# Weight conversion without its clamp, a second load of the weights that checks it, and x of two chunks turned together on VectorE

## The chip, the cores and the metric

One core of one Trainium2 chip. The metric is the device time of one execution in microseconds; the median over several executions is compared with the median of the changed kernel.

## What is computed

A linear recurrence with decay over 768 steps gives x, and a block that mixes over time and then over channels turns x into the output. Everything is float32.

```
r, k, v: (4, 8, 768, 48) = 0.1 * randn      w: the same shape, 0.8 + 0.15 * rand     u: (8, 48)
U: (768, 32)   V: (32, 768)   w_ch1: (384, 1536)   w_ch2: (1536, 384)

for t in range(768):
    y[t]  = r[t] @ (state + (u * k[t]) v[t]^T)
    state = w[t][:, None] * state + k[t] v[t]^T
x = y as (4, 768, 384)
h = x^T @ U @ V;   a = x + h^T;   out = a + relu(a @ w_ch1) @ w_ch2
```

## The kernel before

The 768 steps of each of the four batches are cut into six chunks of 128 steps, 24 chunks (g = 0 to 23) in all. For a chunk, VectorE runs two scans over the decays (steps F and Q), scales r and k by them (RP, KS), TensorE forms the 128 x 128 scores of every head (AM), VectorE merges them under the triangular mask into A (CP), and TensorE multiplies with v (YA) and with the state that the chunk inherits (YZ). ScalarE copies y to a block buffer xT (XE). The state goes on through DS (TensorE), ZA (VectorE) and ZM. For the mixing over time each chunk's x is needed transposed: for chunks 0 to 11 TensorE transposes it (XT, XN), for chunks 12 to 23 VectorE does it in 32 x 32 blocks (XD, 16 instructions of 32 x 96 for a chunk, line 676); k is turned the same way (KD, 16 instructions of 32 x 128).

When a batch's six chunks are there, GA, G4, SELM, GS, GSL form the small product with U, HP multiplies with V, UADD adds it to x, and UH and UL split the sum into a high and a low part, each of which fits TensorE's rounded 32-bit format (fp32r). The feed-forward part runs over seven blocks of 384 or 512 columns (WIDTHS). A block has 12 UP groups (line 826) and 12 DN groups (line 860) of nine matmuls each: high times high, low times high, high times low. HH and HL (lines 831, 833, 837) make the high and low part of the hidden rows, O (875) adds the result, OUT (878) stores it.

The weights come as 64-bit numbers, 27 pieces: U, V in two halves, and 12 pieces each of w_ch1 and w_ch2 (384 KB a piece). The pair of 32-bit words of a number is turned into one float32 by `split_raw`: AB takes the absolute value of the high word (ScalarE, line 271), E scales the low word (ScalarE, 288), C1 clamps (VectorE, 293), C2 shifts (300), C3 puts the sign back (307), ADD adds the low word (GpSimd, 314), HI and SUB split the result into high and low part (324, 331). Data that fall outside what the fast path can do are told by flags (`guard`, `tots`): PW, PC, PD reduce them, PF reads the flag, and a slow general path would follow the fast one.

All of this is a list of 1415 steps. The order in which they are given out, and for some of them which of two engines takes them, is a written-out string, ORDER: each step has a number, and its third digit says the engine and how many idle matmuls TensorE gets before the step (`lead`; line 186). Each engine takes its instructions in that order and waits where data are not there. SyncE issues all loads and stores, in order too. Buffers come from pools with a number of places (20 in `big`, 3 in `ffn`, and so on); a load waits until its place is free.

In this order the first batch's six chunks and the conversion of the first weights come first, then GA to UL of the first block, then UP 0.3. From there the chunks of later batches run between the matmul groups of earlier blocks.

Of the kernel before, what the change touches and what calls it, by code (L numbers as in the profile page):

```python
# [8 lines left out]
F32 = mybir.dt.float32  # L9
# [41 lines left out]
def channel_order():  # L51
# [25 lines left out]
    "2L02T02o06d06e09U0A602X02h02Z02U06+06-02M12p02Y02a09L07M07102V19602b02r07N0AF07002g09S12s02i09h09W09m02j09V0"
    "2k02q03407209T12t09702c07Q07402x02l07309p07502d07609X02m09Y02e19813M02u09n02y09b02v09o19c09i02n13603503D09d0"
    "2+02w19y0C109e09u1A903709f07702-03E03802z09Z07A03909v19w03F09a13003103203G07R03A07B09x09z0780AH13B0CA03H0A10"
    "7O0A203I07U03V03313e07V03N07S07C0AB03J0A303X03C17P1A703W03K07W07T13Y03L1AC03g07D07X1AY08S13P03Q0AE13O0AD0A40"  # L80
    "7G07b03Z09+0AO03R07c0AA13f03S0AI03a03T0C207d0A807E07k03U17Y0AJ07H0Cf03b07l0Ai07m07e0A503c07F03h03i0CB03d1Ah0"
    "7Z0C403j0Ab0AM07I03k07f1AK1AZ0AL17a07t0Ad07g03l0Aj17n0790Cg03m17u0Ae0CV0CC07J07v0CD0AP07o07z07p0C909-07K07w0"
    "D907+0AN0CH0Ak07L07h0Al0AT0C60Ag0A01Am1AU0Af0Ao0Ch0CI0Ac0C707-0CE07x0CJ0AQ0C81An0CW0AV0C307y0AW0Ap0CF07i07j0"
    "Aa0Ci0AR07q0860C-0CY0CK0CZ0800AS1AX0Aq0DA1Ce0Ca0811Ar0Cd0As07r0820Cl0CN0C51D00DB0CG0CL0Cb0CO1D80Cc1At0DC0CM0"
    "Ef08308707s0D20Cj0CP0Au0Av0840Aw0Ax0Cm0DV0D70Cp0Ay0CX0Ck1DY0Az0Cn0Df0880Eg0850D408908C0Cq08D0Co0CQ0Cr0Dg1D50"
    "Cu0De0DW0Dd0E00D30Da0Cv0D61A+0D-0Dh0Dl0Cs0Db0Di08A0A-08E0E20B30B008F0Hg0B10DZ1B40DF0E708I0B70Dm08J0B80DG0Ct1"
    "DH0E40EW0B20E90B50DD1E31Dc1D108K0Ig0B60DE0B90E10BA08L0Cw0E80Dj1EV0DI0BW0E50DL0DJ08M0Dn08G0DM0BK0BL0Cx0BB0E61"
    "8B0EY0BX0JA0BC0Ea0DK0EA0Dk0BM0EZ1Eh0Dp0EB0DO0Eb0EF0DN1DP0BH0BY08H0Dq0JB0BI0Do0Ec1BD0CR0Bc0Bd0BT0BJ08N0EG0Hh0"
    "Hi0H30EC0BN0Hj0ED0H20Be0DQ0Ee0BO0DX0Dr0EH0Cy0BP0EJ0EE0Ds0Ed0H50BU0Du0BV0Ei0Dv0Dt1BE0BQ0Ej0BZ0Dw0EK0DR0EI0BR0"
    "EL0CS0DS0Ih0H61BF0EM0EO0Ba0Bb0EX0EP0Dx0DT0HW0El0BG0Bi0EN1Ek0H70JC0Bf0EQ0Dy0HC0BS0ER0Bg0HA0IA0Em0Bl0Bj0Ii0En0"  # L90
    "HB0Eo0HZ0HD0HX0Ep0Bm0Bh0Bn0CT0H80Bk0Bo0ES0Dz0I00Eq0Ha1Cz0Br0ET0Hk1Er0DU0CU0Bs0Bp0Bt0IB0He0Es0Et0Bu0D+0C+0EU0"
    "HE0Bx0Eu0HI0Ev0Hf0By0H40Ew0HF0Ex0I30HJ0Ey0Ez0H91Bz0E+0HG1I40Bv0F20E-0F30HM0F00F40I90F60B+0F11F70F80F51F91Hb0"
    "HH0IC1B-0HY0FG0Hc0FM0Bw0FN0HN0FA0FH1Hl0FO0ID0FB0FI0Fb0Hm0FV0Jg0I10FW0I50IE0FC0Fc1Ij0Hd1HK0FD0FE0Fd0FX0FJ0HL0"
    "HO0IF0JD0IW0HP1HQ0FF0Bq0Hn0FK0Hq0IZ0G00I80C00FS0FT0I60FL0Hr0I71HR0FU0G10Ho0Fh0FP0IG0FQ0Fi0Hv0Hw0Jh0Hp0Fj0G21"
    "Hs0IK0Fe0Hx0Ib0Fk0FR0Hy0IH0IX0Ff0IL0If0Ic0FY0Fg0FZ0Ia1Ie0JY0I20Fa0G30Fl0Ik0Im0In0Fm0J00Fn0JW0Ji1Fq0Fo0Il0Fr0"
    "JE0J10Fs0II0G40IJ0Ft0Id0G50Jj0J30G80Fw0Ht0G90G60J50Hu1GA0J60Fu0Iq0IM0G71GB1J40IP0Fv0J80IY0IQ0IR0Hz0Io0IN0HS0"
    "Fx0GC0JG0Fy0JZ0Fz0JH0GX0Fp0GD0Ip0JI0Jk0IO1GY0F+0GR0J70F-0Ir0GZ0J90GS0GE0GU0Is0JF1JK0Iv0Jl1Iw0GT0H+0Jb0HT0Jf0"
    "GI0Ix0IS0H-0Iy0GV0JL0GF0GW0Gd0Ge0GJ1It0GK0Jc0Iu1J20GL0Iz0GG0JX0Gf0Je1Jd1JJ0GO0JM0JP0JQ0GP1GH0GQ0Ja1Jm0GM1Ga0"
    "IT0Jn0JN0GN0HU0JR0Gb1Gg0JO1Gc0Gj0IU0Jo0I+0HV0Jp0Gk1I-0Gh0Jq0Gl0Gi0JS0JT0IV0Gm0Jr0Gn0Go0Gp0Js0JU0JV0Gs0Gt0Jt0"
    "Jv0Ju0Jw0Gu0Gq0Jx0Jy0Gv0Jz0J+0Gy0J-0Gw0K00Gz0K30K11K70K40K20G+0K80K50L10L20K90K60G-0KA1H00Ki0Kj1KN0KZ0Kk0KO0"  # L100
# [7 lines left out]
class Buf:  # L108


    def __init__(self, pool):
        self.pool, self.left = pool, 0
# [20 lines left out]
def plan(steps, caps):  # L133


    order, taken, done = [], dict.fromkeys(caps, 0), set()
    for n in range(0, len(ORDER), 3):
        i, how = DIGITS.index(ORDER[n]) * 64 + DIGITS.index(ORDER[n + 1]), DIGITS.index(ORDER[n + 2])
        s = steps[i]
        assert s not in done and done.issuperset(s.after), s.name  # L140
        if how % 2:
            s.eng = s.alt
        s.lead = how // 2
        for buf in s.take:
            taken[buf.pool] += 1
            assert taken[buf.pool] <= caps[buf.pool], s.name
        for buf in s.bufs:
            buf.left -= 1
            taken[buf.pool] -= not buf.left
        done.add(s)  # L150
        order.append(s)
    assert len(order) == len(steps)
    return order
# [3 lines left out]
def rwkv_moe_kernel(ctx, tc, wT, rkT, vN, vS, rkN, uB, uT, uD, U, V, w1, w2, out):  # L157
# [7 lines left out]
    psF = pool("psF", 3, space=PSUM)  # L165
    dram = pool("dram", 1, space=DRAM)
    big = pool("big", BIG_BUFS)
# [953 lines left out]
```

## Time and profile before

| | us |
|---|---|
| median of 3 runs | 464.66 |
| lowest, highest | 462.23, 464.88 |
| the profiled execution | 463.0 |
| its span, first to last instruction | 461.1 |

The profiled execution lies 1.66 us under the median of the runs; 1.9 us of its time lie outside the span. PE is TensorE's matmuls, PEld its weight loads, DVE VectorE, ACT ScalarE, POOL GpSimd, SP SyncE.

### The profile page before, as it was taken

The page shows a single profiled execution, that of the slowest core. Times are in us where ns is not written, and L with a number is a line of the kernel's source. Part 1 is how long each engine was busy: PE and PEld are TensorE (multiplying, and loading weights), DVE is VectorE, ACT ScalarE, POOL GpSimd, SP SyncE. Part 2 cuts the span into 40 slices and gives each one's busy share as a digit, 9 for nine tenths or more (in the row PEclk, how much of TensorE's full clock was granted, in tenths as well). Part 3 has the DMA queues.
Part 4 walks back from the last instruction along what each step waited for, and adds up shares of the span by engine and source line. Part 5 has one row for each costly group of instructions (what it writes and reads, how often), then busy time and mean ns, then how long its engine had stood idle before and what let it go on. Part 6 is the DMA issues. An engine that isn't in the chain of part 4 may idle for free.

```text
span 461.1 us, 9867 instructions
## 1 busy us (share of the span) xinstructions
PE 438.8 (95%) x3917; PEld 371.7 (81%) x3917; DVE 365.3 (79%) x813; ACT 182.0 (39%) x494; POOL 114.2 (25%) x146
## 2 busy tenths in 40 slices
PE   5997998999999979999999999999999999999994
PEld 2776757898999869777786878887877689999994
DVE  8999789999899989999999999689999545313400
ACT  4888678989654425224302232023330002101200
POOL 1221225423275456645402322210000010000000
PEclk9586599999999999999999999999999999999998
DMA  8994724443755445502211321220200000010002
GB/s 277 282 344 149 253 74 139 150 168 118 228 156 185 138 161 181 160 21 81 83 62 30 143 67 47 67 66 25 67 1 1 23 17 8 0 41 17 2 0 75
DMA packets 20213, 47.38 MB, mean 103 GB/s; under 512 B 2432, under 2 KB 7296, under 8 KB 20160
## 3 DMA queue, kind: packets, MB, share of 16 engines
q1 hardware_dynamic: 20160, 46.67, 31.3%
q8 instruction: 33, 0.54, 0.5%
q14 instruction: 20, 0.16, 0.1%
HBM read 41.94 MB, written 4.72 MB: 101 GB/s over the span
## 4 chain that ended last, share of the span: by engine, by line
PE 58%; DVE 29%; ACT 4%; DMA 4%; issue 3%; SPq 1%; POOL 0%; ACTq 0%; DVEq 0%
PE f L860 22%; PE f L826 22%; DVE xn L676 9%; DVE kn L676 4%; DVE hid L837 3%; DMA raw_w<-in_w 2%; DVE F L379 2%; DVE A L547 2%; PE y L614 2%; DVE Q L392 1%; PE dS L556 1%; PE y L624 1%; PE aps L542 1%; DMA w<-in_wT 1%; PE aps L534 1%
## 5 line engine op out<-in xcount | busy, mean ns | idle before, releaser
L826 PE MATMUL f<-u,w1h 128*128 128x384 f32 (+1 forms) x504 | 150.6, 368 | 1.6 <-DVE hid L837 1.5
L860 PE MATMUL f<-hid,w2h 128*128 128x384 f32 (+1 forms) x504 | 149.8, 367 | 0.0
L826 PEld LDWEIGHTS f<-u,w1h 128*128 128x128 f32 x504 | 93.2, 188 | 15.1 <-DVE hid L837 3.0
L860 PEld LDWEIGHTS f<-hid,w2h 128*128 128x128 f32 x504 | 93.3, 188 | 12.3 <-issue 2.3
L860 PE MATMUL f<-hid,w2l 128*128 128x384 f32 (+1 forms) x252 | 91.5, 363 | 0.0
L826 PE MATMUL f<-u,w1l 128*128 128x384 f32 (+1 forms) x252 | 91.4, 363 | 0.0
L831 ACT ACTIVATE hid<-f 128x384 fp32r<-128x384 f32 (+1 forms) x69 | 36.0, 534 | 117.1 <-PE f L826 109.7
L837 DVE SCALAR_TENSOR_TENSOR hid<-f,hid 128x384 fp32r<-128x384 f32 (+1 forms) x84 | 50.1, 607 | 19.5 <-ACT hid L831 18.7
L676 DVE STREAM_TRANSPOSE xn<-xT 32x96 f32<-32x96 f32 x192 | 51.7, 269 | 2.7
L860 PEld LDWEIGHTS f<-hid,w2l 128*128 128x128 f32 x252 | 47.4, 188 | 5.0
L826 PEld LDWEIGHTS f<-u,w1l 128*128 128x128 f32 x252 | 47.4, 188 | 4.4
L676 DVE STREAM_TRANSPOSE kn<-rk 32x128 f32<-32x128 f32 x160 | 48.3, 302 | 2.4
L314 POOL TENSOR_TENSOR cva_w<-cva_w,raw_w 128x384 int32<-128x384 int32 x24 | 28.0, 1175 | 86.0 <-DVE cva_w L307 32.2
L446 ACT ACTIVATE A<-ident,dv 128x128 f32<-128x128 f32 x120 | 37.7, 391 | 1.0 <-DVE dv L491 0.8
L875 DVE TENSOR_TENSOR xT<-f,xT 128x384 f32<-128x384 f32 (+1 forms) x21 | 12.8, 608 | 26.8 <-PE f L860 26.6
L392 DVE TENSOR_TENSOR_SCAN Q<-w,qd 128x516 f32<-128x516 f32 x24 | 30.7, 1277 | 0.2
L379 DVE TENSOR_TENSOR_SCAN F<-w,resets 128x517 f32<-128x517 f32 x24 | 29.5, 1231 | 0.5 <-DMA w<-in_wT 0.4
L453 POOL TENSOR_SCALAR_AFFINE_SELECT A<-dv 128x128 f32<-128x128 f32 (+1 forms) x54 | 16.8, 348 | 42.9 <-DVE dv L432 36.9
L787 ACT ACTIVATE u<-xT 128x384 fp32r<-128x384 f32 (+1 forms) x18 | 10.0, 568 | 40.0 <-DVE xT L782 24.6
L793 POOL TENSOR_TENSOR u<-xT,u 128x512 fp32r<-128x512 f32 (+1 forms) x8 | 9.2, 1153 | 60.6 <-DVE u L789 49.0
L594 ACT ACTIVATE Z<-Z,tots 128x96 f32<-128x96 f32 x64 | 18.6, 363 | 13.4 <-DVE Z L585 13.4
L399 POOL TENSOR_TENSOR rk<-rk,Q 128x512 f32<-128x512 f32 x10 | 11.9, 1190 | 48.2 <-DVE Q L392 44.7
(114 smaller groups left out, 574.2 us busy)
## 6 DMA issues: line engine op xcount, KB each, us to landing
rk<-in_rkT SPq DMA_DIRECT2D x24, 512.0 KB, 5.2
raw_w<-in_w SPq DMA_DIRECT2D x24, 384.0 KB, 4.3
kr<-in_rkN SPq DMA_DIRECT2D x18, 384.0 KB, 3.8
w<-in_wT SPq DMA_DIRECT2D x24, 258.5 KB, 3.0
v<-in_vS SPq DMA_DIRECT2D x24, 224.0 KB, 3.7
out_dram<-xT SPq DMA_DIRECT2D x12, 192.0 KB, 3.3
out_dram<-xT SPq DMA_DIRECT2D x9, 256.0 KB, 2.9
raw_V<-in_V SPq DMA_DIRECT2D x6, 96.0 KB, 6.0
```

The costliest lines, as they stand in the source:

```text
L314: lambda: nc.gpsimd.tensor_tensor(out=d["to"].bitcast(I32), in0=d["a"].bitcast(I32), in1=d["e"], op=ALU.add),
L379: nc.vector.tensor_tensor_scan(out=F[:, ::-1], data0=st["w"][:, ::-1], data1=resets[:, ::-1], initial=1.0, op0=ALU.mult, op1=ALU.add)
L392: nc.vector.tensor_tensor_scan(out=st["Q"], data0=st["w"][:, 0:n], data1=qd, initial=0.0, op0=ALU.mult, op1=ALU.add)
L446: nc.scalar.activation(to, one, AF.Copy, scale=dv[:, NP * i + j : NP * i + j + 1])
L453: nc.gpsimd.affine_select(out=A[:, i, js, ts], in_=dv[:, NP * i + js.start : NP * i + js.stop].unsqueeze(2).broadcast_to([P, NQ, n]), patt ...
L594: nc.scalar.activation(st["Z"][:, j], src[:, j], AF.Copy, scale=nxt[:, j : j + 1])
L676: nc.vector.transpose(a, b)
L826: nc.tensor.matmul(ps, wt[:, f, ct, :], u[ct][:, z], start=(m == 0), stop=(m == 8))
L831: nc.scalar.activation(h[:, 0], d["ps", f], AF.Relu)
L837: nc.vector.scalar_tensor_tensor(out=h[:, 1], in0=d["ps", f], scalar=0.0, in1=h[:, 0].bitcast(F32), op0=ALU.max, op1=ALU.subtract)
L860: nc.tensor.matmul(d["o", ct], wt[:, 4 * ct + part, f - 3 * part, :], hid[f][:, z], start=(part == 0 and m == 0), stop=(part == 3 and m == 8),
L875: nc.vector.tensor_tensor(out=o, in0=d["o", ct], in1=o, op=ALU.add)
```

## The change

1. The conversion loses AB and C1. C2 now reads the high word itself and writes the shifted word to the work buffer; C3 keeps two bits where it kept one. What the clamp did is replaced by a check: 27 steps LCK load each weight piece a second time (384 KB, U 192 KB, V 96 KB each), CK (VectorE) takes the least absolute value of the high words, CM (ScalarE) their sum of absolute values. PW, PC and PD take two more numbers into the flag, and the general path would convert the weights again with the clamp.
2. Where chunks 2n and 2n+1 both belong to VectorE's turning and lie in the same block, their x is turned together after the second one: instructions of 32 x 192 in place of two of 32 x 96. Of the chunks 12 to 23 that makes the pairs 12-13, 14-15, 16-17, 18-19 and 22-23; 20 and 21 lie in different blocks and stay apart. The buffers xn are given out in pairs.
3. Every buffer gets the place that `plan` found free at that point of the list, by name, where before a pool handed places out.
4. Four buffers are taken one step later (dv at DV, kn at KN, hid at HH).
5. ORDER is new for all 1422 steps, with other choices of engine and other idle matmuls. In it GA to UL of the first block come at about the same place; between HP and the first UP (now UP 0.2) stand DS 6, YA 6, AM 7 and XT 1.0, which stood behind the first UPs before. The eleven idle matmuls stand before XT 0.4 and not before the first UP. LCK, CK and CM stand behind two thirds of the list: one piece before the first UP of block 3, the others from there to the end, and PC between the DN groups of the last block.

```diff
+HIGH_MIN, HIGH_END = 1.125 * 2.0**-15, 122880.0
...
-        ab = step("AB " + nm, "ACT", absolute, [l], take=[bcva], use=[braw, bq])
...
-        c1 = step(
-            "C1 " + nm, "DVE",
-            lambda: nc.vector.tensor_scalar(
-                out=d["a"], in0=d["a"], scalar1=2.0, scalar2=122880.0 * 65536.0, op0=ALU.max, op1=ALU.min
-            ),
-            [ab], use=[bcva],
-        )
...
+        def shifted():
+            a = d["a"] = place("cva", [P, cols], f"cva_{kind}_{i}", bcva)[0:m]
...
+            nc.vector.tensor_scalar(
+                out=d["ai"], in0=d["high"], scalar1=3, scalar2=0x3FFFFFFF, op0=ALU.logical_shift_left, op1=ALU.bitwise_and
+            )
...
+        c2 = step("C2 " + nm, "DVE", shifted, [l], take=[bcva], use=[braw, bq])
...
-                out=d["ai"], in0=d["high"], scalar=0x80000000, in1=d["ai"], op0=ALU.bitwise_and, op1=ALU.bitwise_or
+                out=d["ai"], in0=d["high"], scalar=0xC0000000, in1=d["ai"], op0=ALU.bitwise_and, op1=ALU.bitwise_or
...
         for buf in s.take:
-            taken[buf.pool] += 1
-            assert taken[buf.pool] <= caps[buf.pool], s.name
+            buf.slot = free[buf.pool].pop(0)
...
+            def blocks_of_x(i):
...
+                to = both[:, c % 2 + 1 - n : c % 2 + 1]
+                src = blocks[blk][:, :, (cc + 1 - n) * P : (cc + 1) * P].rearrange("p a (n t) -> p n a t", t=P)
+                for j in range(4):
+                    q = slice(32 * j, 32 * j + 32)
+                    r = slice(32 * i, 32 * i + 32)
+                    if n == 1:
+                        nc.vector.transpose(to[q, 0, :, r], src[r, 0, :, q])
+                    else:
+                        nc.vector.transpose(to[q, :, :, r], src[r, :, :, q])
...
+        def again():
+            d["high"] = load_weight(kind, i, 1, b)[1][0:rows].bitcast(F32)
+
+        def least():
+            nc.vector.tensor_reduce(
+                out=ends[0:rows, 0, n : n + 1], in_=d["high"], op=ALU.min, axis=AX.X, apply_absolute_value=True
+            )
+
+        def sizes():
+            x = d["high"]
+            nc.scalar.activation(
+                junk.rearrange("p a b -> p (a b)")[0:rows, 0 : x.shape[1]], x, AF.Abs,
+                accum_out=ends[0:rows, 1, n : n + 1],
+            )
...
-    pw = step("PW", "DVE", worst, guards + [sts[g]["tots"] for g in range(B * NCH)])
+    pw = step("PW", "DVE", worst, guards + looks + [sts[g]["tots"] for g in range(B * NCH)])
```

## Rows read from the trace of the kernel before

**Rows 1.** The page, parts 1 and 2: busy time, its share of the span and the instructions of an engine; then the granted clock of TensorE and the busy share of the DMA engines in 40 slices of 11.5 us, in tenths.

```profile
PE 438.8 (95%) x3917; PEld 371.7 (81%) x3917; DVE 365.3 (79%) x813; ACT 182.0 (39%) x494; POOL 114.2 (25%) x146
PEclk9586599999999999999999999999999999999998
DMA  8994724443755445502211321220200000010002
```

**Rows 2.** The timeline of the chip, in order of time: start, length, engine, line, instruction, what it writes and reads; in brackets the idle time before it. The first weight load of an UP group, and the last VectorE instruction of the program.

```profile
71.73 0.19 PEld L826 LDWEIGHTS f<-u,w1h 128*128 128x128 f32 x1
...
455.31 0.56 DVE L875 TENSOR_TENSOR xT<-f,xT 128x384 f32<-128x384 f32 x1 [5.07 <-PE f L860]
```

**Rows 3.** The chain of work that ended last, in order of time (start, length, what): stretches of UP (L826) and DN (L860) groups, 512 columns wide up to 360 us and 384 wide behind it, and the matmuls of one chunk (aps is AM, dS is DS, the four y are YA and YZ), with one AM of the unswapped form ahead.

```profile
124.53 1.09 PE aps L542 x16
...
255.21 14.70 PE f L826 x63
...
288.48 12.59 PE f L860 x54
...
305.77 0.83 PE aps L534 x32
306.60 0.49 PE dS L556 x16
307.09 0.57 PE y L614 x16
307.67 0.44 PE y L624 x16
308.10 0.44 PE y L637 x16
308.54 0.22 PE y L641 x8
...
436.19 19.10 PE f L860 x108
```

**Rows 4.** Busy time of each engine in the stretch from the first UP to the last VectorE instruction. The first row is of all instructions (PE, PEld, DVE, ACT, POOL, then clock, DMA share, GB/s); the next four are of those alone that touch the tiles trx (XT), trk (KT), ga (GA) and gb (SELM), PE and PEld first.

```profile
71.73:455.31 383.58, 377.58 (x3269) 326.33 (x3267) 300.86 (x697) 128.79 (x339) 98.25 (x124) 1.00 0.25 79
71.73:455.31 383.58, 3.16 (x18) 2.02 (x18) 2.91 (x6) 1.00 0.25 79
71.73:455.31 383.58, 2.40 (x16) 1.99 (x16) 2.94 (x5) 1.00 0.25 79
71.73:455.31 383.58, 6.12 (x36) 1.50 (x36) 1.47 (x3) 1.00 0.25 79
71.73:455.31 383.58, 2.47 (x6) 0.89 (x6) 1.67 (x3) 1.46 (x3) 1.00 0.25 79
```

**Rows 5.** Busy time of each engine in the stretch from the first scan to the first UP, with the same columns, and two idle times of VectorE within it from the timeline.

```profile
3.83:71.73 67.90, 60.68 (x650) 45.11 (x648) 61.63 (x109) 53.14 (x156) 14.08 (x13) 0.72 0.71 238
...
54.49 0.36 DVE L293 TENSOR_SCALAR cva_w<-cva_w 128x384 f32<-128x384 f32 x1 [1.95 <-ACT cva_w L271]
59.26 1.32 DVE L549 COPY_PREDICATED A<-maskf,aps 128x1024 f32<-128x1024 uint32 x1 [2.17 <-PE aps L542]
```

**Rows 6.** Groups of instructions by line and shape: count, busy us, mean ns of one, idle time before them. In this order: the turning of x, the turning of k, C3, RED of a chunk, C1, C2, AB, the two instructions of GUARD (a pass over 512 elements and the read of its accumulator), one SUB and one RP.

```profile
L676 DVE STREAM_TRANSPOSE xn<-xT 32x96 f32<-32x96 f32 x192 | 51.7, 269 | 2.7
L676 DVE STREAM_TRANSPOSE kn<-rk 32x128 f32<-32x128 f32 x160 | 48.3, 302 | 2.4
L307 DVE SCALAR_TENSOR_TENSOR cva_w<-raw_w,cva_w 128x384 uint32<-128x384 uint32 x24 | 13.1, 564 | 0.1
L432 DVE TENSOR_REDUCE dv<-kr 128x8 f32<-128x384 f32 x18 | 9.7, 544 | 0.1
L293 DVE TENSOR_SCALAR cva_w<-cva_w 128x384 f32<-128x384 f32 x24 | 9.3, 393 | 2.0 <-ACT cva_w L271 1.9
L300 DVE TENSOR_SCALAR cva_w<-cva_w 128x384 uint32<-128x384 uint32 x24 | 8.6, 366 | 0.1
L271 ACT ACTIVATE cva_w<-raw_w 128x384 f32<-128x384 f32 x24 | 13.3, 557 | 3.6 <-DMA raw_w<-in_w 2.1 <-DVE w1l L331 1.2 <-DVE w2l L331 0.2
L408 ACT ACTIVATE junk<-w,b_max 128x512 uint8<-128x512 uint32 x24 | 17.2, 715 | 0.0
L408 ACT ACTIVATION_READ_ACCUMULATOR junk<-w,b_max 128x1 f32 x24 | 4.6, 194 | 0.0
L331 DVE TENSOR_TENSOR w1l<-cva_w,w1h 128x384 fp32r<-128x384 f32 x11 | 6.0, 555 | 0.0
L399 DVE TENSOR_TENSOR rk<-rk,Q 128x512 f32<-128x512 f32 x14 | 9.5, 682 | 0.0
```

**Rows 7.** Busy time by stage (columns as in rows 4) in three stretches before the first UP, with the granted clock, and in two stretches of 20 us late in the program.

```profile
37.00:40.00 3.00, 1.12 (x4) 0.72 (x4) 2.94 (x5) 2.18 (x7) 1.70 (x2) 0.64 0.28 79
...
44.00:57.00 13.00, 12.31 (x122) 10.43 (x125) 10.99 (x22) 8.85 (x30) 2.03 (x2) 0.50 0.80 280
...
60.00:72.00 12.00, 11.18 (x118) 6.29 (x117) 11.82 (x23) 9.25 (x25) 4.03 (x3) 1.00 0.44 143
...
340.00:360.00 20.00, 20.00 (x163) 16.09 (x164) 19.16 (x58) 2.76 (x7) 0.00 (x0) 1.00 0.01 2
...
400.00:420.00 20.00, 20.00 (x116) 19.71 (x115) 4.57 (x10) 1.01 (x2) 0.00 (x0) 1.00 0.07 24
```

**Rows 8.** DMA issues by what they move: count, size, median time from issue to landing.

```profile
raw_w<-in_w SPq DMA_DIRECT2D x24, 384.0 KB, 4.3
```

More of the change, by code (lines that the diff above doesn't have):

```diff
@@ L133, in plan @@
 def plan(steps, caps):
-    order, taken, done = [], dict.fromkeys(caps, 0), set()
+    order, done = [], set()
+    free = {pool: list(range(n)) for pool, n in caps.items()}
     for n in range(0, len(ORDER), 3):
@@ L144, in plan @@
         for buf in s.take:
-            taken[buf.pool] += 1
-            assert taken[buf.pool] <= caps[buf.pool], s.name
+            buf.slot = free[buf.pool].pop(0)
         for buf in s.bufs:
             buf.left -= 1
-            taken[buf.pool] -= not buf.left
+            if not buf.left:
+                free[buf.pool].append(buf.slot)
         done.add(s)
@@ L180, in rwkv_moe_kernel @@
     busy = resets.bitcast(BF16)[:, 0:512]
-    idle = psF.tile([P, 512], F32, tag="ffn", name="idle")
+    idle = place("ffn", [P, 512], "idle")
     leading = [0]
@@ L649, in chunk @@
             )
-        blk = max(n for n in range(NB) if STARTS[n] <= g * P)
+        blk = block_of(g)
         cc = g - STARTS[blk] // P
@@ L656, in out_x @@
             if cc == 0:
[L657 removed]
+                blocks[blk] = place("xT", [P, NCT, FB], f"xT_{blk}", xbuf[blk])
             nc.scalar.activation(blocks[blk][:, :, cc * P : (cc + 1) * P], st["y"], AF.Copy)
@@ L690, in turn @@
             for i in range(4):
                 last = [step(
-                    f"XD {b}.{c}", "DVE", lambda i=i: blocks_of_x(i), last, take=[bxn] if i == 0 else [], use=[bx, bxn],
+                    f"XD{n} {b}.{c}", "DVE", lambda i=i: blocks_of_x(i), last,
+                    take=([bxn] if n == 2 else take) if i == 0 else [], use=[bx, bxn],
                 )]
+                d.setdefault("first", last[0])
             d["steps"] = last
+            if n == 2:
+                even["steps"] = last
@@ L1001, in rwkv_moe_kernel, with look @@
                 ffn(blk, lambda ct, blk=blk: flat[ct, :, STARTS[blk] : STARTS[blk] + WIDTHS[blk]])
-    per = const.tile([P, 2], F32, name="per")
+    looks = []
+    ends = const.tile([P, 2, len(pieces)], F32, name="ends")
+    nc.gpsimd.memset(ends, 1.0)
+    def look(n, kind, i):
+        d, b = {}, Buf("big")
+        rows = RANK if kind == "V" else P
+        def again():
[3 more added lines that the diff above has]
+                out=ends[0:rows, 0, n : n + 1], in_=d["high"], op=ALU.min, axis=AX.X, apply_absolute_value=True
+            )
+        def sizes():
[3 more added lines that the diff above has]
+                accum_out=ends[0:rows, 1, n : n + 1],
+            )
+        l = step(f"LCK {n}", "SP", again, take=[b])
+        looks.append(step(f"CK {n}", "DVE", least, [l], use=[b]))
+        looks.append(step(f"CM {n}", "ACT", sizes, [l], use=[b]))
+    for n, key in enumerate(pieces):
+        look(n, *key)
+    per = const.tile([P, 4], F32, name="per")
     low = const.tile([1, 1], F32, name="low")
```

354 lines of the change are left out of this document (197 added, 157 removed).

## The prediction, made before the changed kernel was run

> **What bounds the kernel now.** I read the page first: TensorE is busy 95% of the span, VectorE 79%, ScalarE 39% [rows 1]. These are means over two stages, so I look for where they part. The first UP group loads its first weights at 71.73 us, and the last VectorE instruction starts at 455.31 [rows 2]: 383.6 us lie between.
>
> How much of these 383.6 us must TensorE have? At their best the 512-column groups take 14.70 us for 63 matmuls, 0.233 each, and the 384-column ones 19.10 for 108, 0.177 each [rows 3]. Blocks 2 to 4 have 3 x 216 matmuls of the one width, the other four blocks 4 x 216 of the other: 648 x 0.233 + 864 x 0.177 = 151.2 + 152.8 = 304.0 us. The chunks run between: YA and YZ 0.57 + 0.44 + 0.44 + 0.22 = 1.67 for 15 of them and 1.01 for the three that begin a batch, 28.1; thirteen AM at 0.83 and four at 1.09, 15.2; fifteen DS at 0.49, 7.4 [rows 3]; XT, KT, GA and SELM 3.16 + 2.40 + 6.12 + 2.47 = 14.2 [rows 4]; 18 HP at 0.18 or 0.23, 3.7. Sum 372.6. So only **11.0 us** of the 383.6 are anything but TensorE at its rate, though VectorE is nearly full beside it up to 360 us (19.16 of 20 us at 340 to 360, 4.57 of 20 at 400 to 420 [rows 7]). Behind the first UP, then, TensorE is the bound and can give back 11 us at most.
>
> Before it, VectorE is: 61.63 busy of 67.90 us from the first scan to the first UP, with ScalarE at 53.14 [rows 5] and the DMA engines at 0.8 to 0.9 for the first 37 us [rows 1]. Two of its idle times are named: 1.95 us for AB, 2.17 us for scores [rows 5].
>
> **The conversion.** AB goes, 0.557 each on ScalarE, and C1, 0.393 on VectorE, 27 times [rows 6]: 10.6 us of VectorE in all, 11 x 0.393 = 4.3 of them ahead of the first UP by the order given. C2 now reads every second word of the loaded piece. No row has a one-input pass like that on VectorE. The bounds are C2 over dense data, 0.366, and C3, two inputs with one of them strided, 0.564 [rows 6]. I take 0.37: a stride costs C3 nothing against SUB's dense 0.555 [rows 6]; the other end adds 27 x 0.2 = 5.3 us, 12 x 0.2 = 2.4 before the first UP. The Trainium skill bears on the choice: its page "VectorE: DVE Perf Modes", section "What auto-detection actually checks", lets a one-source 32-bit op take both ports by the dimensions' evenness and asks no unit step. By that rule C2 stays at 0.366 and the sum is as I take it; without it the sum would be 5.3 us larger. No row here shows which.
>
> **Ahead of the first UP.** The freed VectorE time is not left free. Counting both orders up to the last UADD of block 0, VectorE loses eleven C1 (4.3 us) and gains one C2 and one C3 (0.93), two SUB (1.11), one RP (0.68) and one CP (1.32), 4.0 us together [rows 5, 6]. So the first UP comes when it came before, about 71.7. Below this lie the 1.95 us wait for AB, which is gone, and up to 1 us of other idle time; above it the 2.4 us of a slow C2, and XT 1.0, which now stands ahead of UP and waits for XE 6. I take 0, between -3 and +3. What is won is that TensorE has by then done more: DS 6, YA 6, AM 7 and XT 1.0, 0.49 + 1.01 + 1.09 + 0.53 (3.16 / 6) = **3.1 us** [rows 3, 4], in time in which it waited anyway. That counts in full, since all behind the first UP is TensorE's.
>
> **The turning of x.** Five pairs: 160 instructions of 32 x 96 at 0.269 become 80 of 32 x 192. From 96 to 128 columns the time goes from 269 to 302 ns [rows 6], 1.03 a column, so 192 should take 269 + 99 = 368 ns: 43.0 - 29.4 = 13.6 us less. Bounds: nothing saved at 538 ns; 17.9 saved were they at 0.314, just over k's. All of it lies beside TensorE's work. XD2 waits for the second chunk's XE; queued behind it on VectorE are HL steps, for which UP's psum places and DN wait. One such wait of a chunk's matmuls (3.0 us [rows 3]) would cost up to that.
>
> **The check.** 27 CK at a RED's 0.544, 14.7 us of VectorE, and 27 CM at AB's 0.557 plus an accumulator read of 0.194, 20 us of ScalarE [rows 6]. Nearly all stand where ScalarE idles and, from 360 us on, VectorE too [rows 7]; there they cost nothing. Some twelve CK come before that, 6.5 us. The 27 loads take 4.3 us each to land [rows 8] at a time when DMA is 0.01 to 0.07 busy [rows 7]. Behind an LCK that waits for its place stand later loads and OUTs on SP; the last chunks' loads are the ones that could suffer. PC would hold the last DN groups if a look were late; 14 groups of 1.59 us, 22 us, lie between the last LCK and PC, against 4.3 + 0.5. So 0.
>
> **What the relief is worth.** Behind the first UP and up to 360 us VectorE loses 16 x 0.393 + 13.6 = 19.9 us and gains 6.5, and some steps move to it from GpSimd and ScalarE. It is not the bound, so this can only shorten the 11.0 us in which TensorE waits. A fifth of that, **2.1 us**, is my value, between 0 and 7. The tail behind 455.31 stays, as do named places and later-taken buffers: I cost them at 0, hidden by the same places in number; a load that waits longer for its place would cost what an unlucky load does, a few us.
>
> **Sum.** 463.0 (profiled execution) - 3.1 - 2.1 + 0 = 457.8. The median lies 1.66 above that execution, so 459.5 is forecast.
>
> **Rivals.** (a) *VectorE is the bound up to 360 us and its relief counts nearly in full.* For it: 19.16 of 20 us busy [rows 7]. Two thirds of the 11.0 would go: 463.0 - 3.1 - 7.3 = 452.6, median 454. The Trainium skill's page "Perfetto Trace Analysis", section "Identifying the Most-Contended Engine", speaks for it: judge TensorE by its weight loads' share, not by matmul time. By that rule TensorE has 57 us to spare here (326.33 of 383.58 [rows 4]) and VectorE's relief would win all of its 13 us, 447 with the moved work; the trace speaks against it, since a 512-column matmul takes 0.233 us at its best and its load 0.19 [rows 2, 3], so the share cannot pass 0.81 there.
> (b) *Nothing comes through.* The turned pairs cost what two single turns did, or C2 is at 0.56, or new waits of XD2 and CK eat the relief: 463.0 - 3.1 + 2.4, about 462.3, and up to 464 with the new waits: median 464 to 466.
> (c) *Slower: the clock is low when the UPs begin.* The granted clock was 0.50 at 44 to 57 us behind a stretch in which TensorE was busy 1.12 of 3 us, and 1.00 at 60 to 72 where idle matmuls filled the gaps [rows 7]. Now only three idle matmuls stand behind YA 5, where seventeen stood. If it falls to 0.50 for as long as that stretch, 13 us of UPs run at half speed: +6.5. It decides once the clock is under 1.0 at the first UP: 463.0 - 3.1 + 6.5 = 466.4, median 468. Against it: eleven idle matmuls at XT 0.4, and DS 6, YA 6, AM 7 in the gap.
>
> **How the numbers follow.** Forecast 0.50, (a) 0.18, (b) 0.17, (c) 0.15. The forecast's own spread, first UP -3 to +3 and relief 0 to 7, is 453 to 465; the range goes from (a)'s 454, a little below, to near (c): 453.5 to 466.5. About 1%, 4.6 us, is what this kernel's measurement can tell from no change: under 460.0 is faster, over 469.3 slower. The forecast gives just over half of its chance to faster, (a) all, (b) none, (c) a third of its chance to slower and the rest to same, with a little more to slower for loads that come late: faster 0.45, same 0.46, slower 0.09.
>
> **What would show it.** First UP at 69 to 75 us with the clock at 1.0; from there to the last DN about 378 us, the same rates of 0.233 and 0.177; C2 at 0.37, turns at 0.37, CK at 0.54; VectorE's busy time about as before, moved from ahead of 360 us to behind it; PC without a wait before it. A first UP behind 75 us, a clock of 0.5 there, C2 near 0.56, or SP waiting at an LCK with loads behind it would make the prediction wrong.

## The result

The changed kernel takes 448.20 us (447.31 to 448.57, four runs) beside 463.45 (461.63 to 464.88, four runs) for the one before: ratio 0.967 [0.9625, 0.9715], 15.2 us less. All medians below are of the fast runs alone: one of the four runs with a shift of 224 and three of the ten with ScalarE's pass, each over 1.5% above the fastest of its kernel, are left out. The time lies outside the range that was given (453.5 to 466.5). Rival (a), relief of VectorE counted nearly in full, points the right way, though it gave 454.

The profiled execution has a span of 446.3 us where 461.1 stood. The page after: busy times, the granted clock and the DMA share in 40 slices (now of 11.2 us).

```profile
PE 426.4 (96%) x3906; PEld 366.1 (82%) x3906; DVE 362.7 (81%) x750; ACT 189.7 (42%) x533; POOL 104.0 (23%) x123
...
PEclk9996799999999999999999999999999999999998
DMA  8966836244654635331307030174212130133020
```

TensorE is busy 12.4 us less than in [rows 1], with eleven matmuls fewer. So most of the gain was counted as TensorE's busy time before. The two marks between which the prediction counted are the first weight load of UP, here from the timeline, and the last VectorE instruction, here from the chain:

```profile
68.28 0.19 PEld L865 LDWEIGHTS f<-u,w1h 128*128 128x128 f32 x1
```

```profile
439.38 0.56 DVE xT L917
```

The second row is the last of the chain of work that ended last. Against [rows 2] the first UP comes 3.4 us sooner (71.73 to 68.28), the stretch behind it is 12.5 us shorter (383.58 to 371.10), and what follows the last VectorE instruction is 1.1 us longer (5.8 to 6.9): 14.8 us in all, the difference of the spans.

Busy time in that stretch after, columns as in [rows 4]: all instructions, then those alone that touch the tiles aps (AM), dS (DS), y (YA, YZ), trx (XT), ga (GA) and f (UP and DN).

```profile
68.28:439.38 371.10, 366.95 (x3203) 321.27 (x3201) 297.38 (x638) 136.70 (x376) 87.92 (x100) 1.00 0.33 109
68.28:439.38 371.10, 15.16 (x464) 12.80 (x464) 22.38 (x17) 1.00 0.33 109
68.28:439.38 371.10, 8.19 (x224) 6.33 (x224) 7.08 (x13) 2.02 (x8) 1.00 0.33 109
68.28:439.38 371.10, 28.20 (x904) 23.65 (x904) 8.22 (x17) 1.00 0.33 109
68.28:439.38 371.10, 2.78 (x18) 1.91 (x16) 2.93 (x6) 1.00 0.33 109
68.28:439.38 371.10, 4.82 (x36) 1.16 (x36) 1.47 (x3) 1.00 0.33 109
68.28:439.38 371.10, 309.10 (x1512) 269.80 (x1512) 73.37 (x123) 34.65 (x65) 1.00 0.33 109
```

The kernel before, in the stretch of [rows 4]: AM, DS, the y matmuls, UP and DN.

```profile
71.73:455.31 383.58, 16.32 (x480) 13.77 (x480) 23.74 (x18) 1.00 0.25 79
71.73:455.31 383.58, 8.54 (x240) 6.68 (x240) 6.58 (x12) 3.07 (x12) 1.00 0.25 79
71.73:455.31 383.58, 29.29 (x936) 24.48 (x936) 8.69 (x18) 1.00 0.25 79
71.73:455.31 383.58, 316.32 (x1514) 271.94 (x1512) 71.07 (x120) 35.99 (x69) 1.00 0.25 79
```

UP and DN fell from 316.32 to 309.10. The chunk that was moved ahead of the first UP takes 3.0 us out of the stretch: AM 16.32 to 15.16, DS 8.54 to 8.19, the y matmuls 29.29 to 28.20, XT 3.16 to 2.78 [rows 4 for XT and the whole]; XT's three matmuls lie across the first mark, so that a part of them is still counted. GA, which waits for turned x, fell from 6.12 [rows 4] to 4.82. TensorE's idle time fell from 6.0 (383.58 less 377.58 [rows 4]) to 4.15. The largest item is therefore UP and DN themselves: 7.2 us. Most of it is the rate at which their matmuls follow each other, as the section on the place of the buffers shows.

Where VectorE is full has moved too. Two stretches late in the program, before the end of the chunks' work and behind it:

```profile
300.00:320.00 20.00, 18.69 (x260) 14.58 (x259) 19.36 (x49) 9.50 (x27) 1.37 (x1) 1.00 0.43 144
...
340.00:360.00 20.00, 20.00 (x93) 16.84 (x92) 6.41 (x12) 2.94 (x8) 2.00 (x2) 1.00 0.17 57
```

At 340 to 360 us VectorE was busy 19.16 of 20 us before [rows 7] and is at 6.41 now. Its chunk work ends some 20 us earlier.

### The profile page after: what moved, and what is told of

Read it like the earlier page. It is cut to its first block, busy times and chain, and to the rows that moved or that the text cites. A ratio compares the mean times of both kernels' runs of the same rounds, so it can differ in the third digit from the quotient of the medians.

```text
span 446.3 us, 9868 instructions
## 1 busy us (share of the span) xinstructions
PE 426.4 (96%) x3906; PEld 366.1 (82%) x3906; DVE 362.7 (81%) x750; ACT 189.7 (42%) x533; POOL 104.0 (23%) x123
## 4 chain that ended last, share of the span: by engine, by line
PE 40%; DVE 16%; issue 1%; ACT 1%; DVEq 0%
PE f L899 20%; PE f L865 16%; DVE xn L720 5%; DVE kn L685 2%; DVE hid L876 2%; DVE xn L718 1%; DVE A L555 1%; DVE F L387 1%; PE aps L542 1%; DVE Q L400 1%; PE hp L816 1%; DVE xT L917 1%; PE y L622 1%; DVE Z L593 0%; PE y L632 0%
## 5 line engine op out<-in xcount | busy, mean ns | idle before, releaser
L865 PE MATMUL f<-u,w1h 128*128 128x384 f32 (+1 forms) x504 | 147.9, 364 | 1.0 <-DVE hid L876 1.0
L899 PE MATMUL f<-hid,w2h 128*128 128x384 f32 (+1 forms) x504 | 148.3, 364 | 0.0
L870 ACT ACTIVATE hid<-f 128x384 fp32r<-128x384 f32 (+1 forms) x65 | 34.6, 538 | 106.6 <-PE f L865 104.0
L876 DVE SCALAR_TENSOR_TENSOR hid<-f,hid 128x384 fp32r<-128x384 f32 (+1 forms) x84 | 50.2, 606 | 13.4 <-ACT hid L870 12.5
L454 ACT ACTIVATE A<-ident,dv 128x128 f32<-128x128 f32 x148 | 46.6, 391 | 11.7 <-DVE dv L440 3.9
L322 POOL TENSOR_TENSOR cva_w<-cva_w,raw_w 128x384 int32<-128x384 int32 x24 | 26.2, 1100 | 70.1 <-DVE cva_w L315 51.9
L832 POOL TENSOR_TENSOR u<-xT,u 128x512 fp32r<-128x512 f32 (+1 forms) x11 | 13.5, 1236 | 92.0 <-DVE u L828 85.1
L720 DVE STREAM_TRANSPOSE xn<-xT 32x192 f32<-32x192 f32 x80 | 29.6, 370 | 1.3 <-ACT xT L666 0.2
L407 POOL TENSOR_TENSOR rk<-rk,Q 128x512 f32<-128x512 f32 x12 | 16.4, 1365 | 45.0 <-DVE Q L400 42.3
L461 POOL TENSOR_SCALAR_AFFINE_SELECT A<-dv 128x128 f32<-128x128 f32 (+1 forms) x33 | 11.5, 382 | 58.1 <-PE f L865 23.3
L602 ACT ACTIVATE Z<-Z,tots 128x96 f32<-128x96 f32 x60 | 17.5, 364 | 10.3 <-DVE Z L593 10.2
L1088 ACT ACTIVATE junk<-raw_w 128x384 uint8<-128x384 f32 x24 | 13.1, 544 | 19.7 <-DMA raw_w<-in_w 19.5
```

Source lines behind the costliest of these rows:

```text
L322: lambda: nc.gpsimd.tensor_tensor(out=d["to"].bitcast(I32), in0=d["a"].bitcast(I32), in1=d["e"], op=ALU.add),
L454: nc.scalar.activation(to, one, AF.Copy, scale=dv[:, NP * i + j : NP * i + j + 1])
L602: nc.scalar.activation(st["Z"][:, j], src[:, j], AF.Copy, scale=nxt[:, j : j + 1])
L720: nc.vector.transpose(to[q, :, :, r], src[r, :, :, q])
L865: nc.tensor.matmul(ps, wt[:, f, ct, :], u[ct][:, z], start=(m == 0), stop=(m == 8))
L870: nc.scalar.activation(h[:, 0], d["ps", f], AF.Relu)
```

## Experiments

Each run's ratio is to runs of the kernel before on the same chip; its interval is in brackets.

### Undoing one part of the change

The two chunks' x turned by instructions of 32 x 96 again, order and all else as after:

```diff
-                        nc.vector.transpose(to[q, :, :, r], src[r, :, :, q])
+                        for m in range(2):
+                            nc.vector.transpose(to[q, m, :, r], src[r, m, :, q])
```

> The changed kernel, its order kept, with each pair of chunks turned by two instructions of 32 x 96 in place of one of 32 x 192: 80 more instructions, VectorE 160 x 0.269 - 80 x 0.370 = 13.4 us more, all between 130 and 335 us. Theory that TensorE alone is the bound there: under 2 us slower. Rival, VectorE is a bound of its own in part of this stretch: 5 to 13 us slower.

452.52 us, 0.9787 [0.974, 0.9834]: 4.3 us above the changed kernel, 5.4 by the two ratios, with an interval of some 3 us to either side. The turning, grouped by line and shape, and one chunk pair in the timeline:

```profile
L721 DVE STREAM_TRANSPOSE xn<-xT 32x96 f32<-32x96 f32 x160 | 34.4, 248 | 1.2
...
332.61 3.54 DVE L721 STREAM_TRANSPOSE xn<-xT 32x96 f32<-32x96 f32 x16
```

The changed kernel has 29.6 us here (its row stands below). So these turns cost VectorE only 4.8 us more, and all or nearly all of them reach the end. Turns that alternate between the chunks follow each other in 0.221 us (3.54 / 16), where the kernel before needed 0.269 each [rows 6]. The part that was undone is thus smaller than the 13.6 us of the prediction; but at the prediction's price, 2.1 us for 13.4 of VectorE (19.9 less 6.5), it would have cost 0.8 us, and that lies outside the interval. Where the time goes, from the first UP to the last VectorE instruction, all instructions and GA alone:

```profile
68.17:443.46 375.29, 368.34 (x3203) 321.71 (x3201) 302.22 (x718) 136.69 (x376) 88.50 (x100) 1.00 0.33 107
68.17:443.46 375.29, 6.11 (x36) 1.68 (x36) 1.47 (x3) 1.00 0.33 107
```

The stretch is 4.2 us longer. TensorE idles 2.8 us more (6.95 against 4.15), and GA, which waits for the turns, is 1.3 us longer (6.11 against 4.82).

The two passes of the conversion put back at the places of C2 and E, a dense pass like C1 on VectorE, one like AB on ScalarE; then each of them alone:

```diff
+            nc.vector.tensor_scalar(
+                out=d["ai"], in0=d["ai"], scalar1=0, scalar2=0, op0=ALU.bitwise_or, op1=ALU.bitwise_or
+            )
...
+            nc.scalar.activation(junk.rearrange("p a b -> p (a b)")[0:m, 0:cols], x, AF.Abs)
```

> The changed kernel, its order kept, with one idle pass more on VectorE behind each C2 (27 x 0.37 = 10 us, 4.4 of them before the first UP) and one on ScalarE ahead of each E (27 x 0.55 = 15 us), as C1 and AB cost. Their results are not used. Theory that the prelude is VectorE's: first UP 4 us later (72), and behind it up to 3 us of new waits: 5 to 7 us slower. Rival, VectorE is a bound of its own up to 130 us: 10 us or more slower. Rival, the order has room for them: under 2 us slower.

> The changed kernel, its order kept, with the idle VectorE pass behind each C2 alone (27 x 0.37 = 10 us), none on ScalarE. Both passes together cost 11 us. Theory that VectorE is the bound up to 130 us: 8 to 11 us slower than the changed kernel. Rival, ScalarE is: under 4.

> The changed kernel, its order kept, with the idle ScalarE pass ahead of each E alone (27 x 0.55 = 15 us), none on VectorE. Theory that VectorE is the bound up to 130 us: under 3 us slower than the changed kernel. Rival, ScalarE (81% busy up to 60 us) bounds the prelude: 5 us or more, and the first UP later by 3.

| | us | ratio | first UP |
|---|---|---|---|
| both passes back | 459.23 | 0.9933 [0.9907, 0.9959] | 71.1 |
| VectorE's pass back | 456.67 | 0.9865 [0.9828, 0.9903] | 72.5 |
| ScalarE's pass back | 456.44 | 0.9866 [0.983, 0.9901] | 72.1 |

Beside the changed kernel's 448.20 VectorE's pass alone costs 8.5 us, ScalarE's alone 8.2, both 11.0; by the ratios, which go by runs of the same chip, 9.0, 9.1 and 12.2, with intervals of some 2.5 us to either side. The first weight load of UP in the second and the third of them, from the timeline:

```profile
72.47 0.19 PEld L871 LDWEIGHTS f<-u,w1h 128*128 128x128 f32 x1
```

```profile
72.13 0.19 PEld L870 LDWEIGHTS f<-u,w1h 128*128 128x128 f32 x1
```

About 4 us of each lie ahead of the first UP, the rest behind it. VectorE's busy time grows by 10.5 us (362.7 to 373.2) and 8.5 to 9.0 of them come out at the end: this pass counts almost in full. ScalarE's grows by 10.6 (189.7 to 200.3) and 8.2 to 9.1 come out, though it is busy 42% of the span. Probably that is because its pass stands in the conversion's chain, for whose weights the first UP and VectorE's SUB wait; it was not tried apart.

The check left out (no second load, no CK, no CM; PW, PC and PD run on zeros), and buffers handed out by the pools again in place of named places:

> The changed kernel, its order kept, without the 27 second loads, CK and CM (this check of the weights' range is left out). Theory that they lie where VectorE, ScalarE and DMA idle: within 1.5 us of the changed kernel, 447 to 448. Rival, the CK before 335 us compete with HL: 3 us or more faster, out of the 14.7 of VectorE.

> The changed kernel, its order kept, with buffers handed out by the pools as before in place of the named places. Theory that the place's name does nothing by itself: within 1 us of the changed kernel. Rival, it keeps loads and tiles from waiting for a wrong place: 3 us or more slower, with SP or PE waits that the changed kernel does not have.

446.25 us, 0.9667 [0.962, 0.9713], and 446.73 us, 0.9663 [0.9627, 0.97], against 0.967 for the change. Neither makes a difference that can be told; the intervals leave room for some 3 us. In the chain after, the flag's two matmuls stand between DN groups with no wait ahead.

```profile
420.23 7.80 PE f L899 x45
428.03 0.12 PE cnt L1118 x2
428.15 11.14 PE f L899 x63
```

Most CK stand where VectorE idles, but not all. From 130 to 335 us, with the check and without it:

```profile
130.00:335.00 205.00, 201.67 (x2082) 164.94 (x2081) 197.32 (x438) 76.56 (x211) 62.01 (x77) 1.00 0.34 109
130.00:335.00 205.00, 201.98 (x2084) 165.70 (x2083) 191.90 (x423) 71.01 (x190) 61.33 (x76) 1.00 0.27 85
```

These 5.4 us of VectorE (197.32 less 191.90) cost nothing that can be told. What VectorE's time is worth depends on what stands behind it in the list, even where it is 96% busy.

### Doing one part alone

Without the clamp (C1 and AB out, C2 and C3 as after), everything else and the order as before; the weights' check is left out:

> The kernel before, its own order, pools and engines, with AB and C1 left out and C2 and C3 as in the changed kernel; the clamp's part of the computation is left out and nothing checks it. 10.2 us of VectorE and 14.8 of ScalarE less, nearly all before 125 us. Theory that VectorE is the bound up to there, whatever the order: 8 to 10 us faster, about 453. Rival, the new order is what makes use of it: under 4 us faster.

461.40 us, 0.9966 [0.9938, 0.9994]. The passes that cost 11 to 12 us when put back into the new order give 1.6 when taken out of the old one. The two are not quite each other's reverse: VectorE is busy only 4.8 us less here (365.3 to 360.5), where the passes put back made it 10.7 more. A part of the difference is that three of the 24 C2 take 0.97 to 1.19 us where the middle one takes 0.352. Each of the three starts while an instruction of GpSimd (POOL) runs and ends 0.2 us behind it, as here:

```profile
74.57 1.30 POOL L311 TENSOR_TENSOR cva_w<-cva_w,raw_w 128x384 int32<-128x384 int32 x1 [4.85 <-ACT raw_w L287]
74.90 1.19 DVE L297 TENSOR_SCALAR cva_w<-raw_w 128x384 uint32<-128x384 uint32 x1
```

In the new order the longest C2 takes 0.589. The rest is probably the order itself: in a fixed list, an engine that becomes free waits for what the list has next, and the freed time is only worth what another order makes of it.

The old order with all else that could be put in it: no clamp, pairs turned together, buffers moved as in the next section; the weights' check is left out:

> The kernel before, its own order, pools and engines, with the conversion without the clamp, x of two chunks turned together at the second chunk's steps, and the address of u and hid as in the changed kernel; no second load and no check. If the parts add up by themselves, about 463 - 9 - 4 - 4 = 446, and the new order and the named places bring nothing; if the order carries half of it, about 455.

453.54 us, 0.9826 [0.9777, 0.9874]. Its partner is the changed kernel without the check, which has the same parts in the new order: 0.9667 [0.962, 0.9713]. The new order, its choices of engine and the named places together are worth 7.4 us (some 3 to either side), and named places alone nothing. The stretch from the first UP to the last VectorE instruction in the one and in the other, its marks rounded, all instructions:

```profile
69.12:445.92 376.80, 369.82 (x3269) 323.87 (x3267) 284.42 (x600) 121.89 (x323) 97.86 (x124) 1.00 0.25 80
```

```profile
67.40:437.60 370.20, 366.43 (x3203) 321.40 (x3200) 285.45 (x611) 121.29 (x322) 88.00 (x100) 1.00 0.25 82
```

The second has 66 matmuls less here, 64 of them the chunk that was moved ahead, and TensorE is busy 3.4 us less; its TensorE idles 3.8 us in place of 7.0. So about half of the order's 6.6 us in this stretch is moved work, about half fewer waits; 1.7 us more come ahead of the first UP.

### The place of the buffers

The new constants of the check move every buffer behind them by 224 bytes. In the kernel before the rows of u and hid, which UP and DN read as the moving operand, begin 96 bytes behind a multiple of 256, after it 64 bytes. The edit widens one constant; nothing else differs:

```diff
-    flag = const.tile([1, 1], I32, name="flag")
+    flag = const.tile([1, 57], I32, name="flag")[:, 0:1]
```

> The kernel before with 32 bytes more in one constant, so that every buffer behind the constants (u, hid, rk, raw and the rest) lies 32 bytes further on; nothing else. Theory of the address: the nine matmuls of a group read u and hid at addresses that were 32 over a multiple of 64 before and are multiples of 64 after, and that is why a 384-column matmul took 0.177 us before and 0.173 after, a 512-column one 0.233 and 0.229. Then this kernel shows 0.173 and 0.229, and gains 1512 x 0.0037 = 5.6 us (1.2%). Rival, the rate is of the order of the steps or of the neighbours' traffic: 0.177 and 0.233 stay, gain 0.

> The kernel before with 96 bytes more in one constant: u and hid now lie at 64 over a multiple of 128, as in the changed kernel (before: 96 over; with 32 bytes more: 0 over, where a 384-column matmul took 0.175). Theory of the address, by place within 128 bytes: 0.173 and 0.229 a matmul, the time in UP and DN 313 to 306 us, 5 us less behind the first UP, median about 458. Rival, the changed kernel's rate comes from something else than this place: 0.175 to 0.177 stays, and the time of the kernel before.

> The kernel before with 224 bytes more in one constant, so that u and hid lie at 64 over a multiple of 256, exactly as in the changed kernel. So far a 384-column matmul took 0.1733 us at 64 over 256 (changed kernel), 0.1767 at 96 (kernel before, and the changed one shifted, with the same pattern of intervals), 0.1760 at 128, 0.1767 at 192. Theory of the address by place within 256 bytes: 0.1733 and 0.229 here too, 4 to 5 us less behind the first UP, median about 458.5. Rival, the address does nothing in this kernel: 0.176 to 0.177.

> The changed kernel with the same 32 bytes more, so that u and hid lie at 32 over a multiple of 64 again. Theory of the address: 0.177 and 0.233 a matmul, 5.6 us slower than the changed kernel, about 453.8. Rival: 0.173 and 0.229 stay, 448.2.

> The kernel after moved up by 96 bytes, its rows at offset 160 of 256. Offset theory with odd multiples of 32 slow: 0.1767 and 451.5 us. Otherwise 0.1733 and 448.

> The kernel after with every buffer behind the constants moved up by 192 bytes, so that the rows which the UP and DN matmuls read begin at 0 behind a multiple of 256 bytes (64 in the kernel after, 96 in the kernel before). Address theory, the offset decides and only some offsets are quick: the measured ones are 64 (0.1733 us a 384-column matmul), 96, 128 and 192 (0.176 to 0.177). If 64 is quick because it is not a multiple of 128 and not of 32 alone, 0 goes with 128: 0.176, 451 us. If bound by something else than the offset: 0.1733 and 448. A third: 0 is quicker than any, 0.170 or less, 444 or less.

> The kernel after moved up by 224 bytes, its rows at offset 32 of 256. Offset theory: 32 goes with 96, 0.1767 a matmul and 451.5 us, as the shift of 32 gave. If only the order of the buffers or chance made the difference: 0.1733 and 448.

| kernel, shift | offset | us | ratio |
|---|---|---|---|
| before, none | 96 | 463.45 | 1 |
| before, 32 | 128 | 462.01 | 0.9995 [0.9958, 1.0032] |
| before, 96 | 192 | 460.49 | 0.995 [0.9921, 0.9979] |
| before, 224 | 64 | 458.54 | 0.9931 [0.99, 0.9961] |
| after, none | 64 | 448.20 | 0.967 [0.9625, 0.9715] |
| after, 32 | 96 | 451.50 | 0.9755 [0.9715, 0.9794] |
| after, 96 | 160 | 450.32 | 0.9726 [0.968, 0.9772] |
| after, 192 | 0 | 447.90 | 0.9656 [0.9615, 0.9697] |
| after, 224 | 32 | 449.04 | 0.9674 [0.9619, 0.9728] |

The same last groups in three chains, before with a shift of 224, before with a shift of 32, and after with none:

```profile
416.79 15.61 PE f L826 x90
432.40 18.74 PE f L860 x108
```

```profile
417.38 15.84 PE f L826 x90
433.23 19.03 PE f L860 x108
```

```profile
404.62 15.60 PE f L865 x90
```

Two groups of the changed kernel at the offset 0 (shift of 192), 512 and 384 columns wide:

```profile
344.31 14.28 PE f L899 x63
...
405.64 15.63 PE f L865 x90
```

With little else running, 384 columns take 0.1733 us at the offset 64 (15.60 / 90), 0.1737 at 0 and 0.176 at 128; before, at 96, they took 0.177 [rows 3]. A shift of 224 bytes alone makes the kernel before 3.2 us faster, and a shift of 32 makes the changed one 3.3 slower (3.9 by the ratios). So 3 to 4 of the 15 us come from where the new constants happened to push the buffers. The expected rule, that multiples of 128 and odd multiples of 32 are slow, fell: offset 0 is as quick as 64, and 32 and 160 lie between. Which property of the address decides stays open, and so does whether it is the rows of u and hid alone, for every buffer behind the constants moves with them.

UP and DN from the first UP to the last VectorE instruction, in the kernel before at the offset 64 (shift of 224), then in the changed kernel at 96 (shift of 32); the last row is all instructions of the latter:

```profile
69.66:451.16 381.50, 312.65 (x1515) 270.36 (x1512) 71.05 (x120) 35.95 (x69) 1.00 0.25 80
70.34:445.05 374.71, 314.13 (x1512) 272.37 (x1512) 73.62 (x123) 34.70 (x65) 1.00 0.33 108
70.34:445.05 374.71, 371.66 (x3203) 324.02 (x3201) 298.04 (x638) 136.84 (x376) 87.60 (x100) 1.00 0.33 108
```

So of the 7.2 us by which UP and DN fell, the place takes 3.7 (316.32 to 312.65) to 5.0 (314.13 to 309.10), and 2.2 to 3.5 are left for fewer waits.

### Idle matmuls and the clock

All idle matmuls that ORDER puts before steps taken out of the changed kernel:

```diff
-        s.lead = how // 2
+        s.lead = 0
```

> The kernel after without any of the idle matmuls that ORDER puts before steps. Theory that the granted clock in the first 70 us sets the first UP: without them the half-clock time grows from 13.7 us to 30 or more, the first UP comes 2 to 4 us later (70 to 72) and the time is 450 to 452. Rival, VectorE and ScalarE set the first UP whatever the clock: first UP stays at 68 within 1 us, and the time within 2 us of 448.

447.29 us, 0.9657 [0.9614, 0.9701]. The granted clock in slices, and the first weight load of UP:

```profile
PEclk9588699999999999999999999999999999999999
```

```profile
67.25 0.19 PEld L865 LDWEIGHTS f<-u,w1h 128*128 128x128 f32 x1
```

In this execution the clock is at 1.2 GHz for 27 us in the first 70, twice as long as in the profiled one of the changed kernel (13.7), and yet the first UP comes 1 us sooner and the time is the same. The theory that the clock sets the first UP fell; what moves it are the passes of VectorE and ScalarE, as the kernels with the passes put back show. That the idle matmuls are what kept the clock up is not shown either: the mean clock of the four runs is 0.967 to 0.981 without them and 0.967 to 0.985 with them.

## Why the prediction was wrong

The sum by its own terms, beside what the two profiled executions and the runs show:

| term | predicted | measured |
|---|---|---|
| first UP | 0 (-3 to +3) | -3.4 |
| chunk work moved ahead of it | -3.1 | -3.0 |
| place of the buffers | not in the sum | -3.2 to -3.9 |
| relief behind the first UP | -2.1 (0 to -7) | about -6 |
| tail | 0 | +1.1 |
| median above the profiled execution | +1.66 | +0.2 |

The relief is what is left of 12.5 us after 3.0 for the moved work and 3.5 for the buffers, so the terms close by construction: 463.0 - 3.4 - 3.0 - 3.5 - 6.0 + 1.1 = 448.2, where the profiled execution has 448.02 and the median 448.20. A second reading of the relief needs no such rest: with the rows at the same offset, 96, the stretch is 383.58 us before and 374.71 after (the shift of 32), 8.9 less, and 5.9 without the moved work. The relief and the first UP came out at or near the favourable ends of the ranges that the prediction gave them; what carried the time beyond its range is the place of the buffers, which had no term, and the 1.66 us, which was the scatter of three runs. With a fourth run the median before is 463.45, 0.45 above the profiled execution.

**The step that failed first is "only 11.0 us".** The prediction subtracted TensorE's best from the stretch, and took as its best the rates of [rows 3], 0.233 and 0.177; the place of the buffers stood in the sum at nothing. The changed kernel runs the same groups at 0.1733 (above) and 0.229 (12.36 / 54):

```profile
238.75 12.36 PE f L865 x54
```

That is 648 x 0.004 + 864 x 0.0035 = 5.6 us more that could be won, 16.6 in place of 11.0. Dividing a chain stretch by its count gives the rate at which this build ran, not the engine's floor. That a buffer's address enters into it was not considered at all.

**The second is "a fifth".** VectorE was called not the bound behind the first UP, since TensorE was busy 377.58 of 383.58 us [rows 4], and its relief was priced by the waits of the old order. For the old order such a price was not far off. From the kernel before with the shift of 224 to the old order with no clamp and with pairs, at the same offset, VectorE is busy 17.5 us less, and the time falls by 4.9 (0.9931 to 0.9826), three tenths of it:

```profile
PE 431.6 (95%) x3917; PEld 367.2 (80%) x3917; DVE 364.7 (80%) x813; ACT 181.9 (40%) x494; POOL 114.4 (25%) x146
PE 423.8 (94%) x3917; PEld 363.5 (80%) x3917; DVE 347.2 (77%) x706; ACT 170.8 (38%) x467; POOL 113.7 (25%) x146
```

In the new order VectorE's conversion passes and turns count nearly whole: 4.8 us of single turns cost 4.3 to 5.4, 10.5 us of its pass 8.5 to 9.0. Of the latter 6.6 lie behind the first UP, where the stretch of the profiled execution grew by 5.8. So the prediction took a value of the old order for a kernel that comes with a new one, and the order had no term of its own but the moved chunk: 2.1 us were forecast, about 6 were measured. At the same offset about half of these 6 is TensorE's idle time (6.00 to 3.05), the rest its busy time: UP and DN 2.2, GA 1.5 (6.12 to 4.61). The chain after shows how VectorE holds TensorE, in pieces such as these, VectorE instructions in a row, with TensorE taking over only behind them:

```profile
325.16 0.37 DVE xn L720
325.54 0.37 DVE xn L720
...
328.24 0.69 DVE hid L876
...
332.08 0.86 PE ga L762 x4
```

Eight turns of a pair stand there in a row, then one HL, eight more turns, and then GA. TensorE's share of 96% on the page and VectorE's place in the chain are both true: the two engines wait for each other in turn, and a cut of either can shorten the sum. In the new order that is the mechanism of rival (a); its size was also held down by the 11.0. That VectorE was such a bound in the kernel before, as (a) had it, the runs do not bear out. Why the new order makes more of VectorE's time than the old one was not taken apart.

**The third is the first UP "when it came before".** VectorE's steps were counted in and out and came to 0.3 us. ScalarE's part, AB before the weights can be converted, was priced only through one wait of 1.95 us [rows 5]. With the pass of ScalarE alone put back the first UP is at 72.1, with VectorE's at 72.5. One profile is a rough measure of it: among the nine kernels with the new order and without the passes the first UP lies between 67.2 and 70.4, mean 68.2, and among four builds of the kernel before that differ by their buffers' place alone between 68.8 and 71.7, mean 70.2. So about 2 of the 3.4 us are the change, the rest lies within what one execution differs from another. Here too the order counts: with the clamp's passes taken out of the old order the first UP came at 71.2.

**Rival (c)**, a low clock at the first UP, did not occur. The stretch at half speed came earlier and was shorter than in [rows 7], and the clock was back well before the first UP:

```profile
37.00:50.00 13.00, 11.64 (x125) 9.28 (x128) 12.78 (x24) 10.19 (x31) 4.86 (x4) 0.51 0.80 270
50.00:67.00 17.00, 16.71 (x256) 10.98 (x249) 16.57 (x31) 15.30 (x47) 5.47 (x5) 1.00 0.54 179
```

**Prices that were right.** C2 from the strided piece, the pair, CK, CM and its accumulator read, grouped by line and shape:

```profile
L720 DVE STREAM_TRANSPOSE xn<-xT 32x192 f32<-32x192 f32 x80 | 29.6, 370 | 1.3 <-ACT xT L666 0.2
...
L1088 ACT ACTIVATE junk<-raw_w 128x384 uint8<-128x384 f32 x24 | 13.1, 544 | 19.7 <-DMA raw_w<-in_w 19.5
...
L1082 DVE TENSOR_REDUCE ends<-raw_w 128x1 f32<-128x384 f32 x24 | 12.6, 543 | 0.1
...
L302 DVE TENSOR_SCALAR cva_w<-raw_w 128x384 uint32<-128x384 uint32 x24 | 8.3, 359 | 1.1 <-DMA raw_w<-in_w 1.1
...
L1088 ACT ACTIVATION_READ_ACCUMULATOR junk<-raw_w 128x1 f32 x24 | 4.6, 193 | 0.0
```

0.359 where 0.37 was taken, 0.370 where 0.368 was, 0.543 for 0.544, 0.544 for 0.557. The rule of the Trainium skill's page "VectorE: DVE Perf Modes", section "What auto-detection actually checks", asks a one-source 32-bit pass for no unit step where it lets it take both ports; the 0.359 over every second word, beside 0.366 dense [rows 6], agrees. The Trainium skill's page "Perfetto Trace Analysis", section "Identifying the Most-Contended Engine", as rival (a) used it, pointed to VectorE's relief, which came through; its measure, the weight loads' share of TensorE, does not show how much there was to win, for that share is 82% after as it was 81% before. The 447 that (a) drew from it, 448.6 as a median, lies at the measured 448.20 in part by luck: 3 to 4 us of the gain are the buffers' place, of which it knew nothing.

**How the whole divides**, by kernels that differ in one step each, in ratios to the kernel before: buffers' place 1 to 0.9931 (3.2 us), no clamp and pairs in the old order to 0.9826 (4.9), the new order and named places to 0.9667 (7.4), the check to 0.967 (none); the intervals are some 1.4 us to either side for the first and 3 us for the others. That order of the steps is a choice: put back into the new order, the passes alone cost 11 to 12 us. What of the 4.9 is no clamp and what is pairs was measured only at another offset (no clamp 1.6 there), and the new order was not run with the clamp's own instructions and dependences, only with passes of their size.

## What to carry over

Where two engines are both some 80% busy or more and hand work to each other, test the value of one by adding a known pass to it, for busy shares do not tell it: here the engine that seemed hidden counted nearly whole in two places of the new order, and cost nothing that could be told in a third. In a program with a fixed order, removing work can give little until the order is made anew (17.5 us of VectorE taken out of the old order gave 4.9, 10.5 put back into the new one cost 8.5 to 9.0), so predict the order's effect as a part of its own. Before a time per instruction is called the engine's best, look for it in other builds; buffers that move by some bytes changed it by 2% here, and a control that shifts the buffers by the same bytes belongs beside any change that adds a constant.

## What the runs showed of the hardware that was not expected

Matmuls with a moving operand of 128 x 384 started every 0.173 to 0.177 us, by where the buffers lie and with nothing else changed. With the rows of the operand at the offset 64 of 256 bytes it is 0.1733 (15.60 / 90); at 96 it is 0.177, at 128 0.176. At 0 it is 0.1733 to 0.174, and at 32, 160 and 192 the groups of one build lie between 0.173 and 0.177. With 512 columns it is 0.227 at 0 (14.28 / 63), 0.229 at 64 and 0.232 to 0.234 at the other five.

Turns of 32 x 96 on VectorE that alternate between the halves of one target tile start every 0.221 us, where the kernel before has 0.269 each.

The granted clock of the first 70 us was at 1.2 GHz for 10 to 38 us in four profiled executions of the kernel before, three of them with shifted buffers, and the first UP did not follow it. It need not be the shift's doing: the mean clock of 23 executions of the kernel before, unshifted, goes from 0.950 to 0.985.
